# A table of places: re-laying the order of scores, transposes, weighted values and projections in a two-stage attention kernel

## The chip, the cores and the metric

The kernel runs on one core of one Trainium2 chip. The metric is the device time of one launch in microseconds (us); the median of 3 runs of the kernel before is 550.94 us (549.63 to 551.64).

## What is computed

Stage 1 is a causal attention with a window of 64 keys over 8 batches x 8 heads x 576 positions x 64 dimensions. Stage 2 takes its output `x` (8 x 576 x 512) and computes four experts of causal attention over all 576 positions. Each expert has its own projections, and a gate keeps the best two experts of a position.

```python
scores = np.where((rel >= 0) & (rel < 64), scale * q @ k.T, -1e9)
x = softmax(scores) @ v                        # stage 1, per batch and head
logits = x @ w_gate                            # the two largest of four, softmax over them -> w
for e in range(4):                             # stage 2, per batch
    qe, ke, ve = x @ wq[e], x @ wk[e], x @ wv[e]
    a = softmax(causal(scale * qe @ ke.T))
    out += w[:, e] * (a @ ve @ wo[e])
```

## The kernel before

**Stage 1** goes in groups `g` of four tiles (72 groups, 9 to a batch). `s1_qk(g)` (line 154) makes scores on TensorE into a PSUM tile of the tag "s", the masked minimum on VectorE (L164, L172), the exponentials on ScalarE (L174) and the division by the row sum on GpSimd (L179). `s1_t(g)` (line 190) transposes two groups at once (L210, tag "t"), and VectorE multiplies the result by a triangle on its way to SBUF (L214). `s1_av(g)` (line 219) multiplies by the values (L238, tag "o"); ScalarE and VectorE store the result as a rounded part `xh` (L246) and a rest `xl` (L247). At the end of a batch GpSimd copies the last 64 columns of both into `xt` (L254), which holds the remainders of two batches.

**Stage 2** runs over batches `b` and pairs of experts `pr`. `s2_v` (L319 to L321, tag "d") makes values and gate logits, and its fifth block `j = 4` reads `xt`. `s2_gate` is the gate. `s2_k` and `s2_q` project keys and queries in two halves (tag "d"; ScalarE L397, L405, L414, L420, VectorE L406, L415, GpSimd L416). `s2_s(b, pr, k)` makes the scores of bank `k` (0 to 7) on TensorE (L446, L447, L441, tag "s"). VectorE takes the masked minimum (L460), and ScalarE the exponential (L464, and L469 for the last block of queries, after `k = 7`). `s2_w` works out the weights (VectorE L483 to L485), and GpSimd scales the probabilities in place (L489): banks 0 to 2 into the tile `p2_0`, banks 3 to 7 into `p2_1`. `s2_t(b, pr, part, k)` transposes them (L498, L520, tag "t"), and ScalarE copies them to `pt2_0` or `pt2_1` (L505 to L539). `s2_av(b, pr, part)` multiplies by the values (L554, tag "o"; evacuated by L560 and L561). `s2_o(b, j)` is the output projection (L319 to L321, tag "d"), followed by a copy on VectorE (L570) and the store to DRAM.

PSUM has three tiles of tag "s", two of "t", two of "d" and one of "o" (`SB, TB, DB, OB = 3, 2, 2, 1`). Each of `p2_0`, `p2_1`, `pt2_0` and `pt2_1` exists once.

**The order.** Stage 2 is laid out in half steps: half step `n` holds the scores of the pair `n - 1` (counted over batches and expert pairs) and transposes, values and output of the pair before it. The dictionary `POS` gives each kind of work a stretch within its half step, over which its calls are spread evenly. Two digits after a letter are part and pair, so `T01` is the transposes of part 0 of the second pair. The letter `l` stands for pair 0 of an even batch, whose last block waits for the batch after it. Stage 1 has a place every 1/4.5 of a half step, plus three offsets `LAG` for its three functions.

```python
def spread(key, calls):
    lo, hi = POS[key]
    for i, (f, *args) in enumerate(calls):
        it.append((n + lo + (hi - lo) * (i + 0.5) / len(calls), f, args))
...
for _, f, args in sorted(todo, key=lambda x: x[0]):
    f(*args)
```

The calls are made in the order of these numbers. That order is a priority: a scheduler in the language lays out each engine's queue from it, so two calls near each other may be interleaved or change places. On the chip each engine then works through its own queue in that fixed order.

## Time and profile before

| | |
|---|---|
| runs | 549.63, 551.64, 550.94 us; median 550.94 us |
| the profiled execution | 548.42 us; its span from first to last instruction 546.7 us |
| granted TensorE clock, mean over the span | 0.992 |
| busy, share of the span | TensorE matmuls 93%, weight loads 83%, VectorE 81%, ScalarE 69%, GpSimd 49% |
| DMA | 51.25 MB, 94 GB/s in the mean |

TensorE's matmuls are pipelined, so their ends are modelled, and a gap between two of them is shown only where the wait was longer than the pipeline. An engine's idle time counts only where the engine that sets the pace waits for it. TensorE has the largest share, so its waits are read first, stretch by stretch, and then the queue of the engine that ended each wait.

### The profile page before, as it was taken

The page shows a single profiled execution, that of the slowest core. Times are in us where ns is not written, and L with a number is a line of the kernel's source. Part 1 is how long each engine was busy: PE and PEld are TensorE (multiplying, and loading weights), DVE is VectorE, ACT ScalarE, POOL GpSimd, SP SyncE. Part 2 cuts the span into 40 slices and gives each one's busy share as a digit, 9 for nine tenths or more (in the row PEclk, how much of TensorE's full clock was granted, in tenths as well). Part 3 has the DMA queues.
Part 4 walks back from the last instruction along what each step waited for, and adds up shares of the span by engine and source line. Part 5 has one row for each costly group of instructions (what it writes and reads, how often), then busy time and mean ns, then how long its engine had stood idle before and what let it go on. Part 6 is the DMA issues. An engine that isn't in the chain of part 4 may idle for free.

```text
span 546.7 us, 14117 instructions
## 1 busy us (share of the span) xinstructions
PE 510.7 (93%) x4588; PEld 452.3 (83%) x4588; DVE 442.1 (81%) x1922; ACT 378.4 (69%) x1428; POOL 266.5 (49%) x668
## 2 busy tenths in 40 slices
PE   3889997999999999999999999999999999999996
PEld 3778896897898788898898978888889878898874
DVE  4786887798987979889887989989897997765752
ACT  3788797669485875858677584767849476667572
POOL 5576556543565543645366445564446443242330
PEclk9799999999999999999999999999999999999999
DMA  8556235033250315213251332404242101100102
GB/s 286 195 181 211 67 106 163 2 90 110 74 165 25 111 65 174 82 48 90 83 172 47 97 104 91 149 20 131 68 143 74 34 13 58 41 2 20 59 2 96
DMA packets 20634, 51.25 MB, mean 94 GB/s; under 512 B 2768, under 2 KB 3280, under 8 KB 20560
## 3 DMA queue, kind: packets, MB, share of 16 engines
q1 hardware_dynamic: 20560, 50.35, 29.1%
q8 instruction: 36, 0.59, 0.4%
q14 instruction: 38, 0.31, 0.2%
HBM read 40.90 MB, written 9.44 MB: 92 GB/s over the span
## 4 chain that ended last, share of the span: by engine, by line
PE 47%; DVE 24%; ACT 16%; issue 4%; POOL 4%; DMA 3%; POOLq 0%; DVEq 0%; ACTq 0%; SPq 0%
PE o L554 6%; DVE pt L214 6%; PE s L159 6%; ACT p L174 5%; PE t L498 5%; PE o L238 4%; DVE p L460 3%; ACT p L464 3%; PE s L446 3%; DVE sm L164 3%; PE v2ps L319 3%; DMA q<-in_qT_dram 2%; DVE ks L406 2%; PE v2ps L321 2%; ACT p L469 2%
## 5 line engine op out<-in xcount | busy, mean ns | idle before, releaser
L489 POOL TENSOR_SCALAR p<-p,r 128x192 f32<-128x192 f32 (+3 forms) x128 | 73.2, 587 | 62.9 <-DVE r L485 38.3
L159 PE MATMUL s<-k,qbd 128*128 128x128 f32 x576 | 82.3, 286 | 9.7 <-POOL qbd L68 4.8
L179 POOL TENSOR_SCALAR p<-p,st 128x64 f32<-128x64 f32 x216 | 66.5, 330 | 49.1 <-DVE st L177 32.2
L159 PEld LDWEIGHTS s<-k,qbd 128*128 128x128 f32 x576 | 74.8, 200 | 11.5 <-POOL qbd L68 5.5
L460 DVE CUSTOM_DVE_ANT_0 p<-s,causal 128x320 f32<-128x320 f32 (+3 forms) x160 | 73.3, 472 | 12.5 <-PE s L447 10.9
L464 ACT ACTIVATE p<-p,r 128x192 f32<-128x192 f32 (+2 forms) x96 | 53.4, 557 | 41.1 <-DVE r L460 40.7
L174 ACT ACTIVATE p<-p,st 128x64 f32<-128x64 f32 x216 | 72.2, 337 | 12.0 <-DVE p L172 10.6
L214 DVE TENSOR_TENSOR pt<-t,tri 64x512 f32<-64x512 f32 (+1 forms) x120 | 75.9, 633 | 5.0 <-PE t L210 3.2
L164 DVE CUSTOM_DVE_ANT_0 sm<-s,win 128x128 f32<-128x128 f32 x288 | 69.9, 282 | 11.8 <-PE s L159 8.6
L416 POOL TENSOR_SCALAR qs<-qz 64x256 fp32r<-64x256 f32 x64 | 26.4, 413 | 78.4 <-ACT qz L414 55.0
L498 PE MATMUL t<-ident,p 128*128 128x128 f32 x384 | 58.3, 279 | 5.2 <-ACT pt L511 2.3
L446 PE MATMUL s<-ks,qz 128*128 128x256 f32 (+2 forms) x160 | 55.1, 355 | 2.8 <-DVE r L460 2.8
L554 PE MATMUL o<-pt,v 128*64 128x256 f32 (+3 forms) x512 | 54.3, 340 | 2.3 <-ACT pt L522 2.3
L498 PEld LDWEIGHTS t<-ident,p 128*128 128x128 f32 x384 | 42.8, 140 | 14.8 <-POOL p L489 5.9
L554 PEld LDWEIGHTS o<-pt,v 128*64 128x64 f32 x512 | 38.2, 136 | 19.2 <-ACT pt L522 5.3
L68 POOL TENSOR_SCALAR qbd<-q 64x576 f32<-64x576 f32 x58 | 39.0, 672 | 19.2 <-PE s L159 7.2
L447 PE MATMUL s<-ks,qs 128*128 128x256 f32 (+2 forms) x160 | 48.3, 312 | 0.0
L238 PEld LDWEIGHTS o<-pt,v 128*64 128x64 f32 x1152 | 38.1, 140 | 8.7 <-DVE yl L561 1.4
L238 PE MATMUL o<-pt,v 128*64 128x64 f32 x1152 | 44.0, 228 | 1.2 <-DVE xl L247 1.0
L174 ACT ACTIVATION_READ_ACCUMULATOR p<-p,st 128x1 f32 x216 | 40.9, 189 | 0.0
L414 ACT ACTIVATE qz<-qps 64x256 fp32r<-64x256 f32 x64 | 24.1, 377 | 23.9 <-PE qps L321 15.3
L319 PE MATMUL kps<-xh,wkhi 128*128 128x320 f32 (+1 forms) x128 | 39.7, 310 | 0.4 <-DVE ks L406 0.4
(142 smaller groups left out, 1458.8 us busy)
## 6 DMA issues: line engine op xcount, KB each, us to landing
v<-in_vW_dram SPq DMA_DIRECT2D x32, 576.0 KB, 4.2
k<-in_kT_dram SPq DMA_DIRECT2D x32, 320.0 KB, 3.0
q<-in_qT_dram SPq DMA_DIRECT2D x32, 288.0 KB, 2.9
out_dram<-out SPq DMA_DIRECT2D x32, 256.0 KB, 2.2
out_dram<-out SPq DMA_DIRECT2D x8, 128.0 KB, 2.8
pt<-in_wv_dram SPq DMA_DIRECT2D x1, 512.0 KB, 8.1
pt<-in_wk_dram SPq DMA_DIRECT2D x1, 512.0 KB, 7.5
pt<-in_wq_dram SPq DMA_DIRECT2D x1, 512.0 KB, 8.0
```

Source lines behind the costliest of these rows:

```text
L159: nc.tensor.matmul(ps[:, i], lhsT=qbd_buf[p % NQBD][:, b], rhs=pairs[p][1][:, 64 * b:64 * b + 128], start=True, stop=True)
L164: nc.vector.tensor_tensor_reduce(out=sm[:, i].rearrange("r a c -> r (a c)"), in0=ps[:, i], in1=win[:, int(b == 0)], scale=1.0, scalar=3.0e ...
L174: nc.scalar.activation(pt[:, i], pt[:, i], AF.Exp, bias=st[:, 0, i:i + 1], scale=-1.0, accum_out=st[:, 1, i:i + 1])
L179: (nc.vector if g < FIRST and i < 1 else nc.gpsimd).tensor_scalar(pt[:, i], pt[:, i], st[:, 2, i:i + 1], 1.0, op0=OP.mult, op1=OP.mult)
L214: nc.vector.tensor_mul(t[64 * w:64 * w + 64, :n, e], ps[r, :n], tri[r, w, None, :].to_broadcast([64, n, 128]))
L238: nc.tensor.matmul(o[64 * h:64 * h + 64, 4 * (k % 2) + i], lhsT=pairs[p][2][:, h, b], rhs=t[:, i, 64 * h:64 * h + 64], start=True, stop=True)
L446: nc.tensor.matmul(out, lhsT=QZ[pr][:, e, q], rhs=rhs, start=True, stop=False)
L460: nc.vector.tensor_tensor_reduce(out=dst, in0=ps[:, col:col + n], in1=mask, scale=1.0, scalar=3.0e38, op0=OP.add, op1=OP.min, accum_out=least)
L464: nc.scalar.activation(whole, whole, AF.Exp, bias=least, scale=-1.0, accum_out=r2[:, 1, x:x + 1])
L489: nc.gpsimd.tensor_scalar(p, p, r2[:, 3, x:x + 1], 1.0, op0=OP.mult, op1=OP.mult)
L498: nc.tensor.transpose(ps[:, col:col + 128], P2[part][:, at:at + 128], ident)
L554: nc.tensor.matmul(o[64 * h:64 * h + 64, q0:n], lhsT=V2[b % 2][:, c, 2 * pr + h], rhs=PT2[part][:, h, x:x + w], start=c == 0, stop=c == le ...
```

## The change

Only two constants change: the offsets of stage 1 and the places of stage 2. No instruction is added or removed and no tile changes size.

```diff
-LAG = (0.0, 0.085, 0.14)
-POS = {'T00': (0.006, 0.062), 'T01': (0.0, 0.151), 'T10': (0.0, 0.333), 'T11': (0.115, 0.331), 'T1l': (0.35, 0.542), 'A00': (0.046, 0.13), 'A01': (0.15, 0.221), 'A10': (0.368, 0.468), 'A11': (0.35, 0.45), 'A1l': (0.657, 0.7), 'O0': (0.3, 0.55), 'O1': (0.518, 0.918), 'S00': (0.12, 0.453), 'S01': (0.0, 0.281), 'S10': (0.415, 0.815), 'S11': (0.602, 0.891), 'KQ1': (0.0, 1.0), 'V': (0.03, 0.476), 'G': (0.45, 0.46), 'GR': (0.801, 0.811), 'KQ0': (0.45, 0.95), 'VT': (0.046, 0.066)}
+LAG = (0.019, 0.085, 0.089)
+POS = {'T00': (0.016, 0.022), 'T01': (-0.087, 0.164), 'T10': (0.0, 0.51), 'T11': (0.234, 0.391), 'T1l': (0.391, 0.57), 'A00': (0.11, 0.21), 'A01': (0.161, 0.23), 'A10': (0.428, 0.528), 'A11': (0.331, 0.572), 'A1l': (0.852, 0.865), 'O0': (0.133, 0.55), 'O1': (0.518, 0.962), 'S00': (0.168, 0.334), 'S01': (0.017, 0.393), 'S10': (0.366, 0.664), 'S11': (0.691, 1.014), 'KQ1': (0.0, 1.187), 'V': (0.054, 0.5), 'G': (0.45, 0.46), 'GR': (0.781, 0.788), 'KQ0': (0.45, 0.95), 'VT': (-0.05, -0.008)}
```

The key `GR` is read nowhere. Three places show what this does to the queues. In the names that follow, `p1_19` or `s1_46` is stage 1's group 19 or 46; `s2_3_0_4` is batch 3, pair 0, bank 4; `t2_3_1_0_2` is batch 3, pair 1, part 0, call 2.

**GpSimd's queue, where the first remainder `xt` of batch 1 is copied.** Before:

```order
L254 TENSOR_SCALAR xt0_0_646<-xh1_771 128x4x64
L179 TENSOR_SCALAR p1_20_1293<-p1_20_1293,st1_20_1287 128x64 x4
L68 TENSOR_SCALAR qbd1_82<-q11_1527 64x9x64 x2
L416 TENSOR_SCALAR qs1_131<-qz1_129 64x256
L254 TENSOR_SCALAR xt1_0_647<-xl1_772 128x4x64
```

After the change:

```order
L179 TENSOR_SCALAR p1_19_1211<-p1_19_1211,st1_19_1205 128x64 x4
L254 TENSOR_SCALAR xt0_0_646<-xh1_752 128x4x64
L254 TENSOR_SCALAR xt1_0_647<-xl1_753 128x4x64
L179 TENSOR_SCALAR p1_20_1293<-p1_20_1293,st1_20_1287 128x64 x4
L416 TENSOR_SCALAR qs1_131<-qz1_129 64x256
```

The two copies stood seven instructions apart; now one follows the other.

**ScalarE's queue, around the transposes of part 0 of a second pair.** First batch 2; before:

```order
L414 ACTIVATE qz0_128<-qps_3_0_1_3778 64x256 x2
L469 ACTIVATE p2_1_123,r2_2_1_3318<-p2_1_123,r2_2_1_3318 128x576 x2
L511 ACTIVATE pt2_0_124<-t2_2_1_0_0_3832 128x2x256
L174 ACTIVATE p1_43_3810,st1_43_3804<-p1_43_3810,st1_43_3804 128x64 x4
L517 ACTIVATE pt2_0_124<-t2_2_1_0_1_3838 128x2x128
```

After the change:

```order
L414 ACTIVATE qz0_128<-qps_3_0_1_3759 64x256
L511 ACTIVATE pt2_0_124<-t2_2_1_0_0_3807 128x2x256
L174 ACTIVATE p1_43_3791,st1_43_3785<-p1_43_3791,st1_43_3785 128x64 x4
L517 ACTIVATE pt2_0_124<-t2_2_1_0_1_3838 128x2x128
L469 ACTIVATE p2_1_123,r2_2_1_3364<-p2_1_123,r2_2_1_3364 128x576 x2
```

Then batch 3; before:

```order
L469 ACTIVATE p2_1_123,r2_3_1_4309<-p2_1_123,r2_3_1_4309 128x576 x2
L517 ACTIVATE pt2_0_124<-t2_3_1_0_1_4783 128x2x128
L505 ACTIVATE pt2_0_124<-t2_3_1_0_1_4783 64x2x64 x2
L397 ACTIVATE kf_4_1_4833<-kps_4_1_0_4820 128x64
L405 ACTIVATE ks_4_1_4835<-kps_4_1_0_4820 64x320
L174 ACTIVATE p1_52_4755,st1_52_4749<-p1_52_4755,st1_52_4749 128x64 x4
L522 ACTIVATE pt2_0_124<-t2_3_1_0_2_4840 64x64 x2
```

After the change:

```order
L517 ACTIVATE pt2_0_124<-t2_3_1_0_1_4783 128x2x128
L505 ACTIVATE pt2_0_124<-t2_3_1_0_1_4783 64x2x64 x2
L174 ACTIVATE p1_52_4736,st1_52_4730<-p1_52_4736,st1_52_4730 128x64 x4
L522 ACTIVATE pt2_0_124<-t2_3_1_0_2_4791 64x64 x2
L397 ACTIVATE kf_4_1_4837<-kps_4_1_0_4824 128x64
L469 ACTIVATE p2_1_123,r2_3_1_4313<-p2_1_123,r2_3_1_4313 128x576 x2
```

In both batches the two long exponentials (L469) moved from ahead of the copies of the transposes to behind them; in batch 3 they also stand behind L397, which reads the finished key projection `kps_4_1_0`.

**TensorE's queue, in the scores of part 1 of batch 3, pair 0.** Before:

```order
L446 MATMUL s2_3_0_4_4079<-ks_3_0_3618,qz0_128 128x448
L447 MATMUL s2_3_0_4_4079<-ks_3_0_3618,qs0_130 128x448
L159 MATMUL s1_46_4089<-k20_3692,qbd0_81 128x128 x4
L319 MATMUL ops_2_2_4116<-wohi_512,yh0_132 128x512
L320 MATMUL ops_2_2_4116<-wolo_513,yh0_132 128x512
L321 MATMUL ops_2_2_4116<-wohi_512,yl0_134 128x512
L446 MATMUL s2_3_0_5_4112<-ks_3_0_3618,qz0_128 128x320
```

After the change:

```order
L446 MATMUL s2_3_0_4_4079<-ks_3_0_3618,qz0_128 128x448
L447 MATMUL s2_3_0_4_4079<-ks_3_0_3618,qs0_130 128x448
L446 MATMUL s2_3_0_5_4089<-ks_3_0_3618,qz0_128 128x320
L447 MATMUL s2_3_0_5_4089<-ks_3_0_3618,qs0_130 128x320
L159 MATMUL s1_46_4093<-k20_3687,qbd0_81 128x128 x4
L319 MATMUL ops_2_2_4120<-wohi_512,yh0_132 128x512
L446 MATMUL s2_3_0_6_4116<-ks_3_0_3618,qz0_128 128x320
```

Banks 4 and 5, stage 1's group 46 and bank 6 all write tiles of the tag "s", of which there are three. Now four of them start with only one output matmul between.

## Rows read from the trace of the kernel before

**Rows 1.** Busy us (xcount) by stretch: length, TensorE, weight loads, VectorE, ScalarE, GpSimd; clock, DMA.
```profile
80.00:112.00 32.00, 27.29 (x265) 25.47 (x259) 25.21 (x126) 23.46 (x95) 18.84 (x48) 1.00 0.25 78
112.00:240.00 128.00, 124.40 (x1141) 110.91 (x1140) 113.19 (x486) 89.68 (x352) 65.56 (x161) 1.00 0.31 96
240.00:368.00 128.00, 124.24 (x1139) 110.72 (x1138) 113.32 (x486) 89.67 (x352) 65.41 (x161) 1.00 0.31 96
464.00:546.70 82.70, 75.96 (x560) 63.97 (x554) 47.88 (x190) 49.79 (x157) 24.51 (x51) 0.99 0.11 37
```

**Rows 2.** TensorE's waits, 240 to 368 us: us in total, times, longest.
```profile
PE s L446 <- DVE r L460: 0.9, 2, 0.6
PE o L554 <- ACT pt L522: 0.8, 2, 0.4
PE t L498 <- ACT pt L511: 0.7, 1, 0.7
PE t L498 <- POOL p L489: 0.5, 1, 0.5
PE t L520 <- ACT pt L505: 0.5, 1, 0.5
```

**Rows 3.** TensorE's waits, 80 to 112 us.
```profile
PE v2ps L321 <- POOL xt L254: 2.3, 1, 2.3
PE t L498 <- POOL p L489: 1.1, 1, 1.1
PE o L238 <- DVE xl L247: 1.0, 1, 1.0
```

**Rows 4.** TensorE's longest wait, 464 us to the end.
```profile
PE t L520 <- ACT pt L511: 0.7, 1, 0.7
```

**Rows 5.** GpSimd in order of time near 90 us: start, us, instruction [idle before].
```profile
88.44 0.40 POOL L254 TENSOR_SCALAR xt<-xh 128x256 fp32r<-128x256 f32 x1
...
91.96 0.40 POOL L254 TENSOR_SCALAR xt<-xl 128x256 fp32r<-128x256 f32 x1
```

**Rows 6.** ScalarE in order of time, 250 to 253 us (batch 2, pair 1).
```profile
250.43 0.78 ACT L469 ACTIVATE p<-p,r 128x576 f32<-128x576 f32 x1
...
252.08 0.60 ACT L511 ACTIVATE pt<-t 128x512 f32<-128x512 f32 x1
```

**Rows 7.** ScalarE in order of time, 313 to 316 us (batch 3, pair 1).
```profile
313.41 0.78 ACT L469 ACTIVATE p<-p,r 128x576 f32<-128x576 f32 x1
...
314.86 0.18 ACT L469 ACTIVATION_READ_ACCUMULATOR p<-p,r 128x1 f32 x1
```

**Rows 8.** GpSimd in order of time, 316.5 to 319 us.
```profile
316.90 1.47 POOL L489 TENSOR_SCALAR p<-p,r 128x576 f32<-128x576 f32 x2 [0.65 <-ACT p L174]
```

**Rows 9.** TensorE in order of time, 315.5 to 318.3 us.
```profile
315.94 0.33 PE L520 MATMUL t<-ident,px 128*128 128x128 f32 x1 [0.53 <-ACT pt L505]
...
316.55 0.48 PE L319 MATMUL ops<-wohi,yh 128*128 128x512 f32 x1
...
317.93 0.75 PE L554 MATMUL o<-pt,v 128*64 128x320 f32 x2 [0.45 <-ACT pt L522]
```

**Rows 10.** TensorE in order of time, one call of the value product of part 0.
```profile
127.95 1.23 PE L554 MATMUL o<-pt,v 128*64 128x320 f32 x12
```

**Rows 11.** VectorE in order of time, 267 to 271 us (batch 3, pair 0).
```profile
267.09 2.78 DVE L214 TENSOR_TENSOR pt<-t,tri 64x512 f32<-64x512 f32 x4
269.90 0.62 DVE L460 CUSTOM_DVE_ANT_0 p<-s,causal 128x448 f32<-128x448 f32 x1
```

**Rows 12.** TensorE in order of time, 267.5 to 271.2 us.
```profile
268.08 0.36 PE L446 MATMUL s<-ks,qz 128*128 128x448 f32 x1
...
268.49 1.05 PE L159 MATMUL s<-k,qbd 128*128 128x128 f32 x8
269.30 0.48 PE L319 MATMUL ops<-wohi,yh 128*128 128x512 f32 x1
...
270.59 0.42 PE L446 MATMUL s<-ks,qz 128*128 128x320 f32 x1 [0.35 <-DVE r L460]
```

## The prediction

> **What bounds the kernel now.** I read first the busy time of each engine by stretch, then TensorE's waits in the stretches where it idles, and last, for each wait, the queue of the engine that ended it. The table by stretch shows a pattern of 128 us: 112 to 240 us and 240 to 368 us have nearly the same counts and the same busy times within 0.2 us [rows 1]. One such pattern is four half steps, two batches. In it TensorE is busy for 124.3 of 128 us and VectorE for 113.3, ScalarE for 89.7. So TensorE sets the pace with VectorE not far behind, and an order that leaves every instruction as it was can win only what TensorE waits. That is 3.7 us in a pattern, 4.7 us between 80 and 112 us, and 6.7 us from 464 us to the end, much of it the last outputs running dry [rows 1]. The granted clock is 1.00 in all of these, so there is nothing to win or lose there unless long gaps appear.
>
> The waits have names. In a pattern there are five kinds, 3.4 us together [rows 2]. Between 80 and 112 us, where stage 2 starts up, three waits make 4.4 of the 4.7 us [rows 3]. At the end only one is over half a microsecond [rows 4]. A good order removes these without making others as long.
>
> The times in the sum are those of the profiled execution, 548.42 us, which lies 2.5 us under the median of 550.94 us. I take the differences from the first and set them against the second. About 0.5%, 2.75 us, is what a measurement of this kernel can tell from no change.
>
> **Start-up, 80 to 112 us.** The block of values that reads `xt` waits 2.3 us for GpSimd [rows 3]. GpSimd had copied the first half of `xt` by 88.84 us and began the second at 91.96 us; the 3.1 us between went to seven other instructions [rows 5]. In the new queue nothing stands between, so the second copy can come up to 3 us earlier. It still needs the rest `xl` from VectorE, and TensorE now reaches that block sooner, since fewer scores stand ahead of it. The gain is between 0 and 2.3 us; I take 2.0, near the upper end, because the 3.1 us of work in between exceeds the wait. The other two waits (1.1 us for the scaling of probabilities, 1.0 us for `xl` in the value product) keep their causes. The second may grow: the query projection that stood ahead of it now stands behind. One projection is twelve matmuls, 1.5 us by their spacing, which bounds the loss. I take a loss of 0.5 us. Net: **-1.5 us**, between -4.4 and +1.5.
>
> **The repeating pattern.** I go through the five kinds of wait.
>
> - The transposes of part 0 in an even batch, pair 1, wait 0.7 us for L511 [rows 2]. The copy began at 252.08 us because two exponentials started at 250.43 us ahead of it [rows 6]. They move behind it, 1.65 us out of its way: the wait goes, -0.7.
> - In an odd batch TensorE waits 0.53 us for L505 and then 0.45 us for L522 [rows 9]. ScalarE's queue there had the same two exponentials, 313.41 to 315.04 us, ahead of L517 [rows 7], and a key projection's copies ahead of L522. They move behind. In addition, on TensorE most of a key projection now stands between the last transposes and the value product. Both waits go, -1.0.
> - The other 0.3 us for L522 falls on pair 0 of an even batch. The value product's place moves from 0.088 to 0.160 of a half step, and the transposes' last call from 0.053 to 0.021, so the distance grows from 0.035 to 0.139, 1.1 to 4.4 us at 32 us a half step. The scheduler evened out part of that before, so I count half, -0.15.
> - The wait of 0.5 us for GpSimd's scaling (L489) belongs to the late weights `VT`. These move 0.08 earlier, 2.5 us, and their transposes 0.03 later: -0.5.
> - The 0.9 us for VectorE's minima (L460) come from the three "s" tiles all being in use. The new order bunches the scores, so nothing speaks for a gain: 0.
>
> Together -2.35. What is late next is the exponentials themselves. In the odd batch they now wait for the key projection to end, and the transposes of part 1 need them scaled. From the first exponential to the end of the scaling took 313.41 to 318.37 us, 5.0 us [rows 7, 8]. After the projection TensorE has the value product (1.23 us [rows 10]), five output matmuls (three took 316.55 to 317.48 us, so 1.55 for five [rows 9]) and some eight scores and transposes (two scores took 268.08 to 268.49 us [rows 12], and the transposes less, so about 1.1): an estimate of 3.9 us from these rows. So TensorE would wait 1.1 us. But in the old chain 1.9 us lay between the second exponential and the scaling [rows 7, 8], in which VectorE had the multiplies of stage 1 ahead of its three small steps; in the new queue most of these come first. Without 0.9 us of that the wait is 0.2 us. I take 0.6, in the middle, and count it once a pattern.
>
> Net in a pattern -2.35 + 0.6 = -1.75 us. The pattern holds from 112 to 464 us, where stage 1 has run out: 352 / 128 = 2.75 times. This makes **-4.8 us**, between -9.4 (all 3.4 us gone) and the slower case below.
>
> **The end.** From 464 us on stage 1 is done, so the queues are shorter. The 0.7 us for L511 [rows 4] has the same cause as in the pattern; I count most of it, **-0.5 us**, between -0.7 and 0. The last scores come after the same sum of matmuls as before, so the final run of scores, exponentials, transposes and outputs starts no sooner.
>
> Loads and stores are issued in stage 1's order; `LAG[0]` moves all of stage 1 by 0.019 of a half step, 0.6 us, and DMA's share is 0.31 in the pattern [rows 1], so I cost that at nothing: the buffers ahead cover it. If that cover were gone, a score would wait for its keys, and the waits of the pattern show no such case [rows 2].
>
> Sum: -1.5 - 4.8 - 0.5 = -6.8 us, so 541.6 us for an execution like the profiled one, and **544.1 us** against the median.
>
> **The rivals.**
>
> *Slower: the three "s" tiles fill up.* VectorE must take a minimum before TensorE may write that tile again, three tiles on. In the old order bank 5 waited 0.35 us although a stage 1 group and three output matmuls stood between it and bank 4 [rows 12]: the tile was bank 3's, and VectorE was at a multiply of stage 1 (L214) of 2.78 us and then a minimum of 0.62 us [rows 11]. In the new order bank 6 must have bank 4's tile back after bank 5, the group and one output matmul, an estimate of 1.5 us from the spacings: bank 5 at most the 0.41 us of bank 4, the group 0.81 us [rows 12], an output matmul 0.31 us [rows 9]. A VectorE that is just at such a multiply needs 2.78 + 0.62, so TensorE would wait 1.9 us. This decides as soon as VectorE lags by more than 1.5 - 0.6 = 0.9 us when bank 4 is done. Two runs of scores in a pattern (pair 0 of both batches) are drawn together in this way. So 3.8 us come on in a pattern, 1.75 go: +2.05 x 2.75 = +5.6 us, with start-up at its bad end +1.5, and 558.0 us. For it speaks that VectorE is busy for 113.3 of 128 us. Against it speaks that the new queue puts a value product of part 1 and a whole output block between that multiply and bank 4, over 3 us of TensorE's time that ask little of VectorE.
>
> *No change: the waits move.* The waits for L511 and L505 and the 0.9 us for minima end in a PSUM tile coming free, 2.1 of the 3.4 us, and the tiles are as many as before. If each wait only turns up at the next tile of its tag, the pattern keeps its 2.1 us, the -0.65 of the others is eaten by the 0.6 us for the exponentials, and with start-up at -1.5 the time is 549.3 us. The Trainium skill says in "Perfetto Trace Analysis", section "Optimization Strategy", that the same gap repeating on the engine that should be saturated can mean there is too little SBUF or PSUM for the next tile. By that rule this change, which gives no tile more, would leave the 2.1 us standing. The rows are against it for two of the three: the tile was held because a ScalarE copy stood behind two exponentials [rows 6, 7], not because it was in use.
>
> *Faster still: everything goes.* If all waits of the pattern (3.4 x 2.75 = 9.4), of the start-up (4.4) and the one at the end (0.7) go, the gain is 14.5 us: 536.4 us. Against it: scores that are bunched and exponentials that are later make new short waits.
>
> That the change does nothing is ruled out by the queues, which differ on all four compute engines.
>
> **How the numbers follow.** I give my forecast 0.45, the no-change case 0.20, the slower case 0.20 and the larger gain 0.15. The forecast's own spread, with start-up from -3.5 to +1.5 and 0.2 to 1.1 us for the exponentials, is 540.5 to 548.5. The range reaches to the larger gain and up to between no change and the slower case: 536 to 556 us. About a tenth of the chance lies above it and a few hundredths below. Faster by over 0.5% (below 548.2 us) takes the larger gain, nearly all of the forecast and a little of the no-change case: 0.62. Within 0.5%: 0.20. Slower: 0.18.
>
> **What would show it.** Right: in the pattern, L511, L505 and L522 are gone from TensorE's waits, a pattern lasts about 126.2 us, and the second `xt` copy follows the first within 1 us. Wrong: TensorE waits for L460 over 2 us in a pattern (the slower rival), or waits for L489 by 1 us and more in odd batches (the exponentials are too late), or the same total of waits under other names.

## The result, and the profile after

The changed kernel takes **534.37 us** (median; 533.11 to 535.01) against 550.3 us before (549.63 to 551.64): ratio 0.9705, 95% interval 0.9677 to 0.9732, some 16 us less. The forecast of 544.1 us had the sign right and less than half of the size; the time lies 1.6 us below the range.

| | before | after |
|---|---|---|
| profiled execution / its span, us | 548.42 / 546.7 | 534.42 / 532.7 |
| granted clock, mean | 0.992 | 0.994 |
| TensorE busy, us | 510.7 (93%) | 505.3 (95%) |
| VectorE, ScalarE, GpSimd, share | 81, 69, 49% | 83, 71, 50% |

The first thing to see is the third line. Each engine runs as many instructions as before (TensorE 4588 matmuls), and yet TensorE's busy time is 5.5 us shorter; only the other 8.5 us of the 14.0 are idle time that the rows show.

Busy time in one pattern after the change, columns as in [rows 1], whose line from 240 to 368 us it answers to:

```profile
235.20:360.40 125.20, 123.15 (x1139) 109.85 (x1138) 114.02 (x486) 90.12 (x351) 65.16 (x161) 1.00 0.31 98
```

A pattern of two batches lasts 125.2 us, not 128.0 [rows 1]. For the same 1139 matmuls at the same granted clock of 1.00, TensorE's idle time fell from 3.8 to 2.05 us, and its busy time from 124.24 to 123.15 us.

TensorE's waits in one pattern after the change, 235.2 to 360.4 us, which answer to [rows 2]:

```profile
PE o L238 <- DVE yl L561: 0.7, 2, 0.5
PE s L446 <- DVE r L460: 0.5, 1, 0.5
PE kps L319 <- DVE ks L406: 0.3, 1, 0.3
PE s L446 <- DVE st L164: 0.2, 1, 0.2
```

L511, L505, L522 and L489 are gone from this list, L460 is shorter, three small waits are new: 1.7 us in place of 3.4.

TensorE's waits in the start-up, 80 to 112 us, which answer to [rows 3]:

```profile
PE kps L319 <- DVE ks L406: 1.1, 1, 1.1
PE v2ps L319 <- POOL xt L254: 0.6, 1, 0.6
PE v2ps L319 <- DVE qs L415: 0.3, 1, 0.3
PE o L238 <- DVE xl L247: 0.2, 1, 0.2
```

The two copies on GpSimd that stood 3.1 us apart [rows 5] now lie 0.3 us apart, from the end of one to the start of the other. GpSimd in order of time:

```profile
84.26 0.40 POOL L254 TENSOR_SCALAR xt<-xh 128x256 fp32r<-128x256 f32 x1 [0.55 <-ACT xh L246]
84.98 0.40 POOL L254 TENSOR_SCALAR xt<-xl 128x256 fp32r<-128x256 f32 x1 [0.32 <-DVE r L483]
```

And the long exponentials stand behind the first copies of the transposes, the other way round from [rows 6]. In batch 2 that holds for L511 and L517 alone: L505, at 247.31 us, and L522 still come after them. ScalarE in order of time, the same place in batch 2, pair 1:

```profile
242.74 0.60 ACT L511 ACTIVATE pt<-t 128x512 f32<-128x512 f32 x1 [0.80 <-PE t L498]
...
245.53 0.36 ACT L517 ACTIVATE pt<-t 128x256 f32<-128x256 f32 x1
245.79 0.77 ACT L469 ACTIVATE p<-p,r 128x576 f32<-128x576 f32 x1
```

**Where the 14.0 us are.** Three marks on TensorE show it: the first matmul of stage 1's group 12, and the first of the first key projections (pair 0, half 0) of batch 1 and of batch 7. Ahead of each of them the same matmuls have run in both kernels (237, 857 and 4187), so a difference between two marks is no shift of work from one side of a mark to the other. Before:

```profile
40.37 0.38 PE L159 MATMUL s<-k,qbd 128*128 128x128 f32 x2
...
106.17 0.39 PE L319 MATMUL kps<-xh,wkhi 128*128 128x320 f32 x1
...
482.55 0.39 PE L319 MATMUL kps<-xh,wkhi 128*128 128x320 f32 x1
```

After:

```profile
38.71 0.27 PE L159 MATMUL s<-k,qbd 128*128 128x128 f32 x1
...
101.56 0.39 PE L319 MATMUL kps<-xh,wkhi 128*128 128x320 f32 x1
...
469.42 0.39 PE L319 MATMUL kps<-xh,wkhi 128*128 128x320 f32 x1
```

Busy time between the marks, columns as in [rows 1], first before, then after:

```profile
40.37:106.17 65.80, 59.44 (x622) 55.09 (x621) 51.13 (x258) 51.97 (x204) 40.30 (x102) 1.00 0.38 116
106.17:482.55 376.38, 365.82 (x3334) 325.71 (x3332) 327.65 (x1392) 261.38 (x1012) 183.00 (x448) 1.00 0.28 86
```

```profile
38.71:101.56 62.85, 59.18 (x622) 55.01 (x621) 50.03 (x253) 51.18 (x204) 37.60 (x94) 1.00 0.40 122
101.56:469.42 367.86, 362.12 (x3334) 322.75 (x3332) 331.68 (x1396) 263.19 (x1013) 185.62 (x458) 1.00 0.28 88
```

| stretch | before, us | after, us | shorter by | of that, idle | of that, busy | forecast |
|---|---|---|---|---|---|---|
| start to group 12 | 40.4 | 38.7 | 1.7 | 0.5 | 1.1 | 0 |
| start-up: group 12 to batch 1 | 65.8 | 62.9 | 3.0 | 2.7 | 0.3 | 1.5 |
| patterns: batch 1 to batch 7 | 376.4 | 367.9 | 8.5 | 4.8 | 3.7 | 4.8 |
| batch 7 to the end | 64.2 | 63.3 | 0.9 | 0.5 | 0.4 | 0.5 |

Up to group 12 TensorE's queue is the same in both kernels, so the first line isn't the change's.

### The profile page after: what moved, and what is told of

It reads as the page before. It is cut to its first block, busy times and chain, and to the rows that moved or that the text cites. A ratio compares the mean times of both kernels' runs of the same rounds, so it can differ in the third digit from the quotient of the medians.

```text
span 532.7 us, 14137 instructions
## 1 busy us (share of the span) xinstructions
PE 505.3 (95%) x4588; PEld 447.7 (84%) x4588; DVE 444.3 (83%) x1922; ACT 379.3 (71%) x1428; POOL 266.0 (50%) x668
## 4 chain that ended last, share of the span: by engine, by line
PE 56%; DVE 24%; ACT 12%; issue 3%; DMA 3%; POOL 1%; POOLq 0%; DVEq 0%; ACTq 0%; SPq 0%
PE s L159 7%; PE o L238 6%; PE t L498 5%; DVE pt L214 5%; PE o L554 4%; PE s L446 3%; ACT p L174 3%; DVE sm L164 3%; PE s L447 2%; PE ops L321 2%; DMA q<-in_qT_dram 2%; PE v2ps L319 2%; PE qps L319 2%; DVE p L460 2%; PE v2ps L321 2%
## 5 line engine op out<-in xcount | busy, mean ns | idle before, releaser
L179 POOL TENSOR_SCALAR p<-p,st 128x64 f32<-128x64 f32 x216 | 64.1, 318 | 91.8 <-ACT p L464 42.4
L489 POOL TENSOR_SCALAR p<-p,r 128x192 f32<-128x192 f32 (+3 forms) x128 | 75.2, 602 | 44.8 <-DVE r L485 35.1
L159 PE MATMUL s<-k,qbd 128*128 128x128 f32 x576 | 81.3, 284 | 10.5 <-POOL qbd L68 5.7
L174 ACT ACTIVATE p<-p,st 128x64 f32<-128x64 f32 x216 | 72.3, 337 | 23.0 <-DVE p L172 22.4
L159 PEld LDWEIGHTS s<-k,qbd 128*128 128x128 f32 x576 | 74.7, 199 | 11.9 <-POOL qbd L68 6.4
L164 DVE CUSTOM_DVE_ANT_0 sm<-s,win 128x128 f32<-128x128 f32 x288 | 72.7, 283 | 13.1 <-PE s L159 9.2
L214 DVE TENSOR_TENSOR pt<-t,tri 64x512 f32<-64x512 f32 (+1 forms) x120 | 76.1, 634 | 3.3 <-PE t L210 0.6
L460 DVE CUSTOM_DVE_ANT_0 p<-s,causal 128x320 f32<-128x320 f32 (+3 forms) x160 | 72.1, 471 | 7.6 <-PE s L447 5.0
L446 PE MATMUL s<-ks,qz 128*128 128x256 f32 (+2 forms) x160 | 56.3, 361 | 1.3 <-DVE r L460 0.5
L554 PE MATMUL o<-pt,v 128*64 128x256 f32 (+3 forms) x512 | 51.6, 339 | 0.4 <-ACT pt L522 0.2
L554 PEld LDWEIGHTS o<-pt,v 128*64 128x64 f32 x512 | 35.4, 136 | 18.6 <-issue 1.7
L498 PEld LDWEIGHTS t<-ident,p 128*128 128x128 f32 x384 | 44.0, 141 | 7.2 <-POOL p L489 3.6
L68 POOL TENSOR_SCALAR qbd<-q 64x576 f32<-64x576 f32 x58 | 38.9, 670 | 20.6 <-DMA q<-in_qT_dram 9.7
L238 PEld LDWEIGHTS o<-pt,v 128*64 128x64 f32 x1152 | 37.0, 137 | 9.8 <-DVE yl L561 4.2
L238 PE MATMUL o<-pt,v 128*64 128x64 f32 x1152 | 42.8, 226 | 2.3 <-DVE yl L561 1.6
L319 PE MATMUL kps<-xh,wkhi 128*128 128x320 f32 (+1 forms) x128 | 40.1, 314 | 2.5 <-DVE ks L406 2.5
L174 ACT ACTIVATION_READ_ACCUMULATOR p<-p,st 128x1 f32 x216 | 40.6, 188 | 0.0
## 6 DMA issues: line engine op xcount, KB each, us to landing
out_dram<-out SPq DMA_DIRECT2D x8, 128.0 KB, 2.9
```

Of the source, the lines that this page charges most:

```text
L159: nc.tensor.matmul(ps[:, i], lhsT=qbd_buf[p % NQBD][:, b], rhs=pairs[p][1][:, 64 * b:64 * b + 128], start=True, stop=True)
L164: nc.vector.tensor_tensor_reduce(out=sm[:, i].rearrange("r a c -> r (a c)"), in0=ps[:, i], in1=win[:, int(b == 0)], scale=1.0, scalar=3.0e ...
L174: nc.scalar.activation(pt[:, i], pt[:, i], AF.Exp, bias=st[:, 0, i:i + 1], scale=-1.0, accum_out=st[:, 1, i:i + 1])
L179: (nc.vector if g < FIRST and i < 1 else nc.gpsimd).tensor_scalar(pt[:, i], pt[:, i], st[:, 2, i:i + 1], 1.0, op0=OP.mult, op1=OP.mult)
L214: nc.vector.tensor_mul(t[64 * w:64 * w + 64, :n, e], ps[r, :n], tri[r, w, None, :].to_broadcast([64, n, 128]))
L238: nc.tensor.matmul(o[64 * h:64 * h + 64, 4 * (k % 2) + i], lhsT=pairs[p][2][:, h, b], rhs=t[:, i, 64 * h:64 * h + 64], start=True, stop=True)
```

## The experiments

Two theories stood at the outset. **A**, the forecast's: only waits that the rows show can be won, and each edit has a price of its own. **B**: TensorE's busy rows hide short waits. From the first results came **I** (the places are worth something only together) against **P** (each group of places has its own worth, and these add). The diffs show only the entries of `POS` or `LAG` that differ from the kernel named. In the tables a pattern runs from the first scores of stage 1's group 44 to those of group 62 (before: 128.1 us; after: 125.3), and "busy" is TensorE's in it (124.3 and 123.2).

### One part of the change alone

**Scores.** Against the kernel before:

```diff
-'S00': (0.12, 0.453), 'S01': (0.0, 0.281), 'S10': (0.415, 0.815), 'S11': (0.602, 0.891)
+'S00': (0.168, 0.334), 'S01': (0.017, 0.393), 'S10': (0.366, 0.664), 'S11': (0.691, 1.014)
```

> The kernel before with the four places of the scores (S00, S01, S10, S11) of the change and nothing else. On ScalarE this alone puts the two long exponentials L469 behind the copies of the transposes of part 0. Theory A (as predicted: only TensorE's visible waits can be won): L511, L505 and L522 leave TensorE's waits, 1.7 us less in a pattern, 0.6 comes back for the late exponentials; TensorE's busy time in a pattern stays at 124.2 us; with the end -3.5 us, ratio 0.994. Theory B (busy rows hide short waits): the same waits go and TensorE's busy time of the same 1139 matmuls falls by about 1 us as well: -8 us, ratio 0.986. Theory C (the bunched scores need the other parts of the change, or the three s tiles fill up): waits for L460 grow by over 1 us in a pattern, ratio 1.000 or above.

**Projections and values.** Against the kernel before:

```diff
-'O0': (0.3, 0.55), 'O1': (0.518, 0.918), 'KQ1': (0.0, 1.0), 'V': (0.03, 0.476)
+'O0': (0.133, 0.55), 'O1': (0.518, 0.962), 'KQ1': (0.0, 1.187), 'V': (0.054, 0.5)
```

> The kernel before with the places of the output projection (O0, O1), the second key and query projections (KQ1) and the values (V) of the change and nothing else. The two xt copies stand side by side in GpSimd's queue; the exponentials L469 stay ahead of the copies. Theory A: only the start-up gains, the 2.3 us wait for the xt copy falls to 0.3, a pattern stays at 128.1 us: -2.0 us, ratio 0.996. Theory B: projections that are spread wider also stand between waits of the pattern and shorten it by up to 1 us, visible or not: -4.8 us, ratio 0.991.

**Stage 1's offsets and the late block.** Against the kernel before:

```diff
-LAG = (0.0, 0.085, 0.14)
+LAG = (0.019, 0.085, 0.089)
-'VT': (0.046, 0.066)
+'VT': (-0.05, -0.008)
```

> The kernel before with the offsets of stage 1 (LAG) and the place of the late block VT of the change and nothing else. Theory A: VT takes the 0.5 us wait for L489 out of each pattern, the offsets do nothing: -1.4 us, ratio 0.9975. Theory B: the value product of stage 1 comes 1.6 us earlier and its tile o is free sooner, so a pattern also loses up to 1 us of waits that the rows do not show: -4 us, ratio 0.993.

**Short exponentials.** Against the kernel before, in `s2_s`; it leaves out the exponential of 512 of 576 columns:

```diff
-                whole = P2[1][:, row(4, e):row(4, e) + 576]
+                whole = P2[1][:, row(4, e):row(4, e) + 64]
```

> The kernel before in its own order, where the two exponentials of the last block of queries (L469) work on 64 of 576 columns; the others keep their raw scores. It leaves out most of that block's exponential. What stands ahead of the copies of the transposes is then short. Theory A: the visible waits for L511, L505 and L522 go, 1.8 us in a pattern, TensorE's busy time in a pattern stays at 124.2 us: with the end -5.5 us, ratio 0.990. Theory B: TensorE's busy time falls by 0.5 to 1 us in a pattern as well: -7 to -8.5 us, ratio 0.985 to 0.987. If a wait only moves on to the next tile: within 1 us of before.

The start-up column runs from the first of the three marks above to the second (before: 65.8 us; after: 62.9).

| kernel | median us | ratio to before, 95% | start-up us | pattern us | busy us |
|---|---|---|---|---|---|
| scores alone | 556.66 | 1.0117 (1.0088 to 1.0147) | 63.6 | 131.5 | 126.8 |
| projections, values alone | 550.25 | 1.0003 (0.9985 to 1.0021) | 63.2 | 128.9 | 125.0 |
| offsets, VT alone | 556.14 | 1.0110 (1.0079 to 1.0141) | 66.7 | 130.4 | 125.0 |
| short exponentials | 543.95 | 0.9895 (0.9865 to 0.9925) | 62.7 | 127.7 | 123.9 |

None of the three parts gains anything alone, two lose 6 us each, and the pattern is longer in all three. Theory A's prices don't hold. The waits say how. TensorE's waits with the scores alone, one pattern:

```profile
PE t L498 <- POOL p L489: 1.2, 2, 0.9
PE o L554 <- ACT pt L522: 0.8, 2, 0.5
PE s L159 <- DVE st L164: 0.8, 1, 0.8
...
PE t L498 <- ACT pt L511: 0.2, 1, 0.2
```

The exponentials did go behind the copies, and L511 and L505 fell from 0.7 and 0.5 to 0.2 us each, as forecast. But the transposes of part 1, still at their early place, now wait for the scaling of the later scores (L489), and stage 1's scores wait for VectorE's minima (L164): 0.8 us once in a pattern, so 0.8 of the 2.2 us that the text on scores and part 1 below gives for L164 and L460 are a wait at the pattern's edge counted twice. L522 kept its 0.8 us although no long exponential stands ahead of it any more, so to move these wasn't enough. In batch 3 its copy starts at 321.78 us, right behind the key projection's copies L397 and L405 (from 321.34 us on).

The projections alone do what was forecast for `xt`. TensorE's waits in that kernel, 60 to 121.2 us:

```profile
PE s L446 <- DVE r L460: 1.2, 1, 1.2
...
PE v2ps L319 <- POOL xt L254: 0.2, 1, 0.2
```

The 2.3 us for `xt` [rows 3] and another 0.3 near by are down to 0.2, and the start-up is 2.6 us shorter. But the same places make the patterns longer, by 2.7 us between the second mark and the third (379.1 for 376.4 us), and the end by 1.1. That eats the gain. With offsets and VT alone TensorE waits 1.9 us for L489 and 1.0 us for `xt` in a pattern; that the late block is early there while its weights and its `xt` are not is a reading of the places.

The short exponentials are inconclusive for L511. The kernel is 6 us faster, but the pattern is only 0.4 us shorter, and L511 still waits 0.9 us in it (0.7 before). Of the profiled execution's gain 3.1 us lie in the start-up, where no wait for `xt` is left although no place had moved. The language's scheduler had laid out other queues for the shorter instructions: right ahead of L511's wait in batch 2 stand three matmuls of a key projection, not nine as before, so TensorE came to the transposes earlier by about as much as the copy did. The edit didn't change one thing alone.

### The change without one part

**Old part 0.** Against the changed kernel:

```diff
-'T00': (0.016, 0.022), 'T01': (-0.087, 0.164), 'A00': (0.11, 0.21), 'A01': (0.161, 0.23)
+'T00': (0.006, 0.062), 'T01': (0.0, 0.151), 'A00': (0.046, 0.13), 'A01': (0.15, 0.221)
```

> The changed kernel with the old places of transposes and values of part 0 (T00, T01, A00, A01). Theory I (the places work only together): some 1 us comes back in a pattern, mostly waits for L522 and L505 since the value product again follows its transposes closely; ratio to the kernel before 0.975 to 0.98 (the full change: 0.9705). Theory P (each group of places has its own worth and they add): scores alone +6.4, stage 1's offsets with VT +5.8, projections 0 against -16 for all leaves -28 us for both parts of the transposes, so without part 0 the ratio is near 1.00.

**Old part 1.** Against the changed kernel:

```diff
-'T10': (0.0, 0.51), 'T11': (0.234, 0.391), 'T1l': (0.391, 0.57)
-'A10': (0.428, 0.528), 'A11': (0.331, 0.572), 'A1l': (0.852, 0.865)
+'T10': (0.0, 0.333), 'T11': (0.115, 0.331), 'T1l': (0.35, 0.542)
+'A10': (0.368, 0.468), 'A11': (0.35, 0.45), 'A1l': (0.657, 0.7)
```

> The changed kernel with the old places of transposes and values of part 1 (T10, T11, T1l, A10, A11, A1l), which come earlier, while the scores stay late. Theory I: the transposes of part 1 again wait for GpSimd's scaling L489, 1.2 us and more in a pattern, and TensorE's busy row of a pattern rises by 1 us or more: ratio 0.98 to 0.99. Theory P: part 1 carries about half of -28 us: ratio near 1.00. If the later scores don't need the later transposes: 0.97.

**Old offsets and VT.** The `LAG` and `VT` of the diff above, set back in the changed kernel:

```diff
-LAG = (0.019, 0.085, 0.089)
+LAG = (0.0, 0.085, 0.14)
-'VT': (-0.05, -0.008)
+'VT': (0.046, 0.066)
```

> The changed kernel with the old offsets of stage 1 (LAG) and the old place of the late block VT. Theory I: the wait of 0.5 us for L489 comes back in each pattern and the offsets cost up to 1 us: ratio 0.975 to 0.98. Theory P: what cost 5.8 us alone is taken out: ratio 0.960.

**Old projections and values.** Set back in the changed kernel:

```diff
-'O0': (0.133, 0.55), 'O1': (0.518, 0.962), 'KQ1': (0.0, 1.187), 'V': (0.054, 0.5)
+'O0': (0.3, 0.55), 'O1': (0.518, 0.918), 'KQ1': (0.0, 1.0), 'V': (0.03, 0.476)
```

> The changed kernel with the old places of projections and values (O0, O1, KQ1, V). Theory I: the block that reads xt, now early, waits for the two xt copies again, 2 us in the start-up and 0.5 to 1 us in each pattern, and bunched scores wait for L164 and L460 as in the run with the scores alone (2.2 us in a pattern): ratio 0.98 to 0.985. Theory P: nothing, as it was worth nothing alone: ratio 0.9705.

**Old scores.** Set back in the changed kernel:

```diff
-'S00': (0.168, 0.334), 'S01': (0.017, 0.393), 'S10': (0.366, 0.664), 'S11': (0.691, 1.014)
+'S00': (0.12, 0.453), 'S01': (0.0, 0.281), 'S10': (0.415, 0.815), 'S11': (0.602, 0.891)
```

> The changed kernel with the old places of the scores (S00, S01, S10, S11). The exponentials L469 stand ahead of the copies again in even batches. Theory I (the places work only together): the waits for L511 and L505 come back, 1 to 1.5 us in a pattern, ratio to the kernel before 0.980 to 0.985. Theory P (what a group does alone it does here too): without the 6.4 us that the new scores cost alone, ratio 0.959.

**Old VT alone.** Set back in the changed kernel:

```diff
-'VT': (-0.05, -0.008)
+'VT': (0.046, 0.066)
```

> The changed kernel with the old place of the late block VT alone. With the old offsets of stage 1 as well the ratio was 0.9934, and the new wait there was 2.0 us in a pattern for the minima of stage 1 (L164) at a score tile. If the offsets carry that cost: only the wait of 0.5 us for L489 comes back, 1.4 us in all, ratio 0.973. If VT carries it: 0.99.

| changed kernel with old ... | median us | ratio to before, 95% | pattern us | busy us |
|---|---|---|---|---|
| (nothing) | 534.37 | 0.9705 (0.9677 to 0.9732) | 125.3 | 123.2 |
| part 0 | 541.29 | 0.9851 (0.9821 to 0.9882) | 127.5 | 123.9 |
| part 1 | 547.57 | 0.9960 (0.9941 to 0.9978) | 128.9 | 125.1 |
| offsets, VT | 545.77 | 0.9934 (0.9907 to 0.9960) | 128.5 | 124.2 |
| projections, values | 543.46 | 0.9887 (0.9861 to 0.9914) | 126.9 | 123.9 |
| scores | 546.58 | 0.9948 (0.9924 to 0.9972) | 128.0 | 123.8 |
| VT | 537.82 | 0.9803 (0.9774 to 0.9832) | 125.7 | 123.8 |

Every part is needed, and each of the five groups costs more when left out than theory I expected (projections at the upper edge of it): 0.015 to 0.026. Projections that brought nothing alone (1.0003) are worth 0.018 here. Theory P is out.

The waits didn't always come back where theory I put them. With the old part 0, L522 is back with 0.9 us in a pattern, but in batch 3 the two long exponentials stand ahead of its copy there (314.42 to 315.94 us), so this run doesn't tell the distance between transposes and value product from ScalarE's queue. With the old part 1 it isn't L489 that TensorE waits for: stage 1's value product (L238) waits 0.8 us for L561 and 0.8 us for L214, and L511 is back with 0.7 us, though no long exponential stands right ahead of it. With the old projections `xt` costs 1.1 us in the start-up, but in the pattern the waits are for L406 (1.1) and L489 (0.9), not for `xt`, L164 and L460. With the old scores two long exponentials stand ahead of L511 again in batch 2 (from 251.65 us on), and yet L511 waits only 0.4 us in a pattern and L505 not at all; L460 (1.4) and L415 (0.8) cost more. With the old VT no wait for L489 of 0.2 us or more is in the pattern, so the forecast's -0.5 for that edit had the wrong cause too.

### Two and three parts together

**Scores and part 1.** The new `S`, `T1` and `A1` entries in the kernel before:

```diff
+'S00': (0.168, 0.334), 'S01': (0.017, 0.393), 'S10': (0.366, 0.664), 'S11': (0.691, 1.014)
+'T10': (0.0, 0.51), 'T11': (0.234, 0.391), 'T1l': (0.391, 0.57)
+'A10': (0.428, 0.528), 'A11': (0.331, 0.572), 'A1l': (0.852, 0.865)
```

> The kernel before with the new places of the scores and of transposes and values of part 1 together (S and T1, A1), nothing else. The scores alone gave 1.0117, with 1.2 us in a pattern for L489 and 2.2 us for L164 and L460 at score tiles. Theory I1 (later scores need later transposes of part 1, and that is the core of the change): L489 goes from TensorE's waits and TensorE's busy row of a pattern falls to about 124: ratio 0.985 to 0.99. Theory I2 (the stage 1 offsets and projections must move too, since score tiles wait for L164): only L489 goes, ratio 1.000 to 1.005.

**All of attention.** The same and the new part 0:

```diff
+'T00': (0.016, 0.022), 'T01': (-0.087, 0.164), 'A00': (0.11, 0.21), 'A01': (0.161, 0.23)
```

> The kernel before with all new places of scores, transposes and value products of stage 2, parts 0 and 1 (S, T0, A0, T1, A1); offsets of stage 1, VT and projections stay old. If these three are the change and the rest trims it: ratio 0.98. If each of the rest is needed as the leave-outs say (+0.023 without offsets and VT, +0.018 without projections, and these two overlap little): ratio 1.00 to 1.01.

The pair gave 552.25 us, ratio 1.0054 (1.0032 to 1.0077), and L489 fell from 1.2 to 0.4 us in a pattern: I2. All of attention gave 551.6 us, 1.0044 (1.0023 to 1.0066). Its price with those of the other two parts alone, 0.0044 + 0.0110 + 0.0003, would make 1.016. Together they make 0.9705, so 0.045, some 25 us, lie in how the parts meet.

The longest wait in both kernels is one and the same. TensorE with all of attention, batch 4, pair 1 (between the banks stands a key projection):

```profile
369.35 1.05 PE L159 MATMUL s<-k,qbd 128*128 128x128 f32 x8
370.16 0.45 PE L446 MATMUL s<-ks,qz 128*128 128x448 f32 x1
...
372.29 0.36 PE L446 MATMUL s<-ks,qz 128*128 128x448 f32 x1
372.50 0.37 PE L447 MATMUL s<-ks,qs 128*128 128x448 f32 x1
372.79 1.15 PE L238 MATMUL o<-pt,v 128*64 128x64 f32 x32
375.36 0.41 PE L446 MATMUL s<-ks,qz 128*128 128x320 f32 x1 [1.42 <-DVE st L164]
```

Two banks (L446) fill two of the three "s" tiles; the third holds the scores of stage 1's group 60 (L159). VectorE meanwhile:

```profile
370.94 0.69 DVE L214 TENSOR_TENSOR pt<-t,tri 64x512 f32<-64x512 f32 x1
...
372.02 0.69 DVE L214 TENSOR_TENSOR pt<-t,tri 64x512 f32<-64x512 f32 x1
...
373.10 0.34 DVE L378 COPY g<-gt 64x2 f32<-64x2 f32 x2
373.47 0.42 DVE L415 TENSOR_TENSOR qs<-qps,qz 64x256 fp32r<-64x256 f32 x1
373.81 0.27 DVE L164 CUSTOM_DVE_ANT_0 sm<-s,win 128x128 f32<-128x128 f32 x1
```

The minima of that group begin 4.5 us after its scores, behind the triangle multiplies and the gate's small steps. That is close to the slower rival's mechanism: VectorE at L214 while three "s" tiles are full, only that the tile asked for is stage 1's. L446 waits for L164 by 2.0 us in a pattern with the pair, with all of attention, and with the old offsets and VT in the changed kernel. In the changed kernel the gate's steps are done before the multiplies, and the minima follow 3.4 us after the scores (at 357.26 us):

```profile
355.85 0.34 DVE L378 COPY g<-gt 64x2 f32<-64x2 f32 x2
...
358.86 1.40 DVE L214 TENSOR_TENSOR pt<-t,tri 64x512 f32<-64x512 f32 x2
...
360.63 0.27 DVE L164 CUSTOM_DVE_ANT_0 sm<-s,win 128x128 f32<-128x128 f32 x1
```

### Which offset

In the code `LAG[1]` and `LAG[2]` are added to `LAG[0]`, so setting back `LAG[0]` moves all three functions of stage 1, not its scores alone as the first expectation's name for it suggests.

```diff
-LAG = (0.019, 0.085, 0.089)
+LAG = (0.0, 0.085, 0.089)
```

> The changed kernel with the old offset of stage 1's scores alone (LAG[0] = 0). Value products of stage 1 still stand ahead of bank 4 in TensorE's queue. If the value product's offset is what keeps the score tiles free: no wait for L164 over 0.3 us, ratio to the kernel before 0.970 to 0.977. If the scores' own offset does it: 2.0 us for L164 in a pattern, ratio 0.99.

```diff
-LAG = (0.019, 0.085, 0.089)
+LAG = (0.019, 0.085, 0.14)
```

> The changed kernel with the old offset of stage 1's value product alone (LAG[2] = 0.14). In TensorE's queue the value product of group 56 stands again between banks 4 and 5 of batch 4, pair 1, and not ahead of bank 4, so bank 5 asks for the tile of stage 1's scores 1.1 us sooner. If that decides: the wait for L164 is back, 1.4 us at that place and 2.0 us in a pattern, ratio 0.985 to 0.99. If not: 0.971 to 0.975.

```diff
-LAG = (0.019, 0.085, 0.089)
+LAG = (0.030, 0.085, 0.089)
```

> The changed kernel with all of stage 1 0.011 of a half step (0.35 us) later still: LAG[0] = 0.030. If later is better without end: the remaining 0.7 us in a pattern for L561 and the 0.5 for L460 shrink, ratio to the kernel before 0.965 to 0.969. Theory I (a tuned place, worse on both sides): a new wait of a microsecond or more in a pattern, ratio 0.975 to 0.985.

```diff
-LAG = (0.019, 0.085, 0.089)
+LAG = (0.010, 0.085, 0.089)
```

> The changed kernel with LAG[0] = 0.010, about half way between old (0) and new (0.019). In TensorE's queue the value product of group 56 already stands behind the second key projection, as in the changed kernel. If that place decides: no wait for L214 over 0.3 us in a pattern, ratio 0.970 to 0.974. If the loss follows the offset evenly: 0.978.

| LAG[0], LAG[2] | median us | ratio to before, 95% | pattern us | longest kind of wait in a pattern, us |
|---|---|---|---|---|
| 0, 0.089 | 544.24 | 0.9874 (0.9848 to 0.9901) | 127.7 | L238 for L214, 1.2 |
| 0.010, 0.089 | 542.52 | 0.9875 (0.9855 to 0.9896) | 127.9 | L446 for L164, 1.0 |
| 0.019, 0.089 (the change) | 534.37 | 0.9705 (0.9677 to 0.9732) | 125.3 | L238 for L561, 0.7 |
| 0.030, 0.089 | 539.29 | 0.9821 (0.9800 to 0.9841) | 127.0 | L319 for L406, 1.1 |
| 0.019, 0.14 | 536.97 | 0.9733 (0.9706 to 0.9761) | 125.6 | L319 for L406, 0.5 |

`LAG[0]` decides, and by 0.6 us of stage 1's place against stage 2: 0.0169 or 9 us. With it at 0 the minima of group 60 again begin 4.5 us after their scores, as with both old offsets. The wait for L164 itself isn't in the list with either offset set back alone; TensorE then meets other ones. The expectation that the value product's own offset decides fell: with it set back the product again stands between banks 4 and 5, and TensorE doesn't wait for L164; its 0.0028 can't be told from nothing, as the intervals overlap. Nor is it a matter of later being better. On both sides of the changed value the time is longer, and each time another engine's queue is what TensorE meets. With `LAG[0]` at 0, TensorE's waits in a pattern:

```profile
PE o L238 <- DVE pt L214: 1.2, 2, 0.9
PE o L238 <- DVE yl L561: 0.8, 1, 0.8
PE t L520 <- ACT pt L511: 0.5, 1, 0.5
```

The value product stands ahead of part of the key projection here and comes to L214's multiplies too early. At 0.010 it stands behind the projection, as in the change, and the wait for L214 is down to 0.3 us, but L164 has 1.0; at 0.030 the key projection waits for L406.

### One more move

Both against the changed kernel:

```diff
-'A00': (0.11, 0.21)
+'A00': (0.2, 0.3)
```

> The changed kernel with the value product of part 0, pair 0, later (A00 from 0.11, 0.21 to 0.2, 0.3). Stage 1's value product o1_36 and o1_54 waits 0.7 us in a pattern for L561, which empties the tile o after it. If that wait can be taken out by moving one product: -0.7 us in a pattern, ratio to the kernel before 0.967. Theory I: other waits take its place, ratio 0.971 or above.

```diff
-'KQ0': (0.45, 0.95)
+'KQ0': (0.47, 0.97)
```

> The changed kernel with the first key and query projections 0.02 of a half step later (KQ0 from 0.45, 0.95 to 0.47, 0.97). In TensorE's queue stage 1's value product then begins ahead of the second key projection, which waits 0.3 us in a pattern and 1.1 us in the start-up for L406. If those go: -1.9 us, ratio 0.967. Theory I: other waits take their place, ratio 0.971 or above.

The first gave 540.87 us, 0.9805 (0.9779 to 0.9831): L561's wait fell from 0.7 to 0.2 us in a pattern, and a new one of 0.7 us for L527 took its place. The second gave 536.11 us, 0.9719 (0.9691 to 0.9746), not to be told from the change: the wait of 0.3 us for L406 is gone and the busy row is 0.4 us longer. No kernel of this study is faster than the changed one.

### What the busy rows hide

TensorE near the wait for L511 in the kernel before:

```profile
250.46 0.39 PE L319 MATMUL kps<-xh,wkhi 128*128 128x320 f32 x1
250.69 0.31 PE L320 MATMUL kps<-xl,wkhi 128*128 128x320 f32 x1
...
251.56 0.31 PE L320 MATMUL kps<-xl,wkhi 128*128 128x320 f32 x1
251.71 0.31 PE L321 MATMUL kps<-xh,wklo 128*128 128x320 f32 x1
252.73 0.44 PE L498 MATMUL t<-ident,p 128*128 128x128 f32 x2 [0.71 <-ACT pt L511]
```

Within a projection these matmuls start 0.145 us apart, and a row lasts 0.31. After the last one the next could have started at about 251.86, an estimate from that spacing; it started at 252.73. It lost 0.87 us, and the row shows 0.71. So a wait behind such a matmul is about 0.16 us longer than its row says, and one shorter than that would show no idle time at all. Over the 20 kernels a pattern lasts 125.3 to 131.5 us; TensorE's idle time in it goes from 1.7 to 5.4 us and the busy time of the same 1138 matmuls, at a clock of 1.00, from 123.2 to 126.8 us. With the scores alone:

```profile
255.00:386.50 131.50, 126.77 (x1138) 110.73 (x1138) 114.62 (x486) 90.73 (x351) 65.27 (x160) 1.00 0.29 93
```

Of its 6.2 us over the changed kernel 3.5 are "busy". That the busy time of the same matmuls depends on the order is thus measured; that hidden waits are the reason, as theory B says, is not. A rival stands in the rows above: the first matmul of the projection, behind another kind of work (at 250.46 us), has a row of 0.39, 0.08 us more than those behind it. Between the marks on batches 1 and 7 TensorE's work changes its kind 440 times before, 436 times after the change and 505 times with the scores alone. By an estimate from these rows, 69 changes at 0.08, some 5.5 of the 9.3 us of busy time by which the scores alone exceed the changed kernel there can be that. It explains next to nothing of the change's own 3.7 us, with 4 changes fewer. More can be read in the weight loads, which have rows and waits of their own. Weight loads in the pattern before, 249.6 to 377.7 us:

```profile
PEld s L446 <- DVE r L460: 2.2, 4, 0.8
PEld o L554 <- ACT pt L522: 1.6, 3, 0.9
PEld t L498 <- POOL p L489: 1.2, 2, 0.7
```

L460 has 2.2 us in four waits there and 0.9 us in two in the matmuls' own rows [rows 2]; after the change it has 1.2 us in two there and 0.5 in one. Not every wait of a weight load delays a matmul, so these aren't prices. No run made a short wait on purpose, so how much of the busy time is such waits stays a reading.

## Why the prediction was right and wrong

**The step that failed** is the premise drawn from the bound. That TensorE sets the pace held: it is busy 95% of the span now. But that such an order "can win only what TensorE waits" did not: of the 12.4 us that the change won behind group 12, 4.4 came out of TensorE's busy rows, 3.7 of them in the patterns, where the forecast counted none. The rows of waits put the loss too low. What in the busy rows became shorter stays open.

**The size.** The profiled execution came out at 534.42 us, 7.2 under the forecast's 541.6 for one: about 1.7 from the start, 1.5 from the start-up, 3.7 from the patterns and 0.4 from the end. Against the median 2.5 us more are missing, since the profiled execution before was that much under its median and the one after is at its own. The lower end of the forecast's own spread comes to 541.0 by its terms, not 540.5, and the clock of the last stretch was 0.99, not 1.00; neither matters here.

**Start-up, -1.5 forecast, -3.0 measured.** The `xt` copies came together and their waits, 2.6 us in all, fell to 0.6: the -2.0 was right. The other two waits didn't keep their causes: the 1.1 us for L489 went, and the wait for `xl`, put down for 0.5 us more, fell from 1.0 to 0.2. New waits took some 1.2 us, the longest of them 0.7 us for L68.

**Patterns, -4.8 forecast, -8.5 measured.** The idle part fell by just 4.8 us, but that agreement is partly luck. In one pattern L511 and L505 went, and the scores alone bring each down to 0.2 us, with the exponentials behind the copies as forecast. In the company of the other new places the exponentials don't decide: L511 waits 0.4 us with them ahead of it (old scores) and 0.7 without (old part 1). L522's wait depends on part 0's places and on what stands ahead of its copy. In batch 3 the four exponentials of stage 1 (L174), which the forecast didn't count, took most of that time before, 316.35 to 317.68 us. The term of 0.5 us for L489 and VT had the wrong cause. The +0.6 for late exponentials didn't come; with the transposes of part 1 at their old place and the new scores alone, the wait for L489 rises by 0.7. And L460 gained 0.4 us where none was expected, while L561, L406 and L164 took 1.2.

**A second step that failed** is the one on the offsets: "`LAG[0]` moves all of stage 1 by 0.019 of a half step, 0.6 us, ... so I cost that at nothing". It looked at loads alone. Stage 1's place against stage 2 decides what TensorE finds on VectorE's queue, and set back alone it costs 9 us. That is no share of the 16 us: by the same test each of the five groups costs 8 to 14.

**The rivals.** The slower rival named nearly the right mechanism and about its size (1.9 us forecast for one wait; 1.42 measured in the row above). It happens with the new scores and both old offsets. "The waits move" was true of each part by itself, 1.0003 to 1.0117; in the full change the three waits for PSUM tiles that it kept, 2.1 us, fell to 0.5 with the same tiles. By the rule that its text took from the Trainium skill's "Perfetto Trace Analysis", section "Optimization Strategy", 2.1 us would have stood without more PSUM; here the repeating gaps came from the order of the queues. The larger gain came nearest in time, 536.4 us, but not by its mechanism: 1.7 us of waits remain in a pattern, and the rest came out of busy rows and the start.

**What none of the steps allowed for** is that prices of places don't add. Every term was costed with all other queues as they were, then summed.

## What to carry to other kernels

Where an order of work has been fitted as a whole, the worth of one place taken alone says nothing about its worth among the others: cost an edit with its partners in place, and test it both alone and left out. Shown idle time of the busiest engine is no ceiling on what an order can win; compare busy time of the same instructions between orders, and look at the weight loads' waits. To see where a change won its time, set marks ahead of which the same work has run in both kernels. An offset that shifts a whole stage is an edit on every queue: find the second busiest engine's longest run of work, and ask who needs a tile back while it lasts.

## What the runs showed of the hardware

The start varies by itself. Up to group 12 TensorE's queue is the same in the kernel before, in the changed kernel, with the scores alone and with `LAG[0]` at 0, and yet that group's scores start at 40.37, 38.71, 41.81 and 44.71 us. The granted clock goes with it. First 40 us, changed kernel:

```profile
0.00:20.00 20.00, 10.37 (x60) 9.34 (x60) 11.53 (x60) 9.51 (x36) 13.57 (x54) 0.83 0.82 288
20.00:40.00 20.00, 17.53 (x199) 15.17 (x197) 17.42 (x92) 18.26 (x65) 12.30 (x32) 1.00 0.54 169
```

With `LAG[0]` at 0:

```profile
0.00:20.00 20.00, 10.26 (x44) 9.34 (x44) 11.05 (x59) 9.15 (x35) 12.99 (x53) 0.80 0.81 288
20.00:40.00 20.00, 16.50 (x145) 14.72 (x145) 13.81 (x69) 14.50 (x50) 10.53 (x28) 0.76 0.39 124
```

TensorE is busy for about half of the first 20 us in both, and a part of the time at the lower of its two levels, 1.2 GHz. The two profiled executions that have all of that part in the first 20 us, 0.83 and then 1.00, start group 12 earliest of the 20: the changed kernel at 38.71 us and the one with `LAG[0]` at 0.030 at 39.49. TensorE waits in those 20 us anyway; in the second 20 us the lower level delayed the rest. A profiled execution's difference of a few us between kernels can therefore be the start alone; the medians over several runs are less open to that.
